# Filler matmuls joined to 512 columns and the first load split by head, in a fused attention and MLP kernel

## The chip, the cores and the metric

The kernel runs on one core of one Trainium2 chip. The core has five engines that run side by side and meet at semaphores: TensorE (PE in the profile; its weight loads are PEld), VectorE (DVE), ScalarE (ACT), GpSimd (POOL) and SyncE (SP). Sixteen DMA engines move data between the device memory and the on-chip memory. The metric is the device time of one execution in microseconds (us), as the median over runs.

## The reference

Two attentions in a row, and an MLP on what they give. For each of 8 batches and 8 heads, 32 queries p attend to 576 keys and values, and then the 576 queries q attend to the 32 rows that came out:

```python
def sm_attn(qq, kk, vv):
    s = scale * np.matmul(qq, kk.transpose(0, 1, 3, 2))
    a = np.exp(s - np.max(s, axis=-1, keepdims=True))
    a = a / (np.sum(a, axis=-1, keepdims=True) + 1e-09)
    return np.matmul(a, vv)
p_packed = sm_attn(p, k, v)              # p: (8, 8, 32, 64); q, k, v: (8, 8, 576, 64), all float32
out = sm_attn(q, p_packed, p_packed)
x = out.transpose(0, 2, 1, 3).reshape(4608, 512)
h = x @ w_in                             # (4608, 2048)
g = np.where(h >= 1, h, np.where(h <= -1, 0, (h + 1) ** 2 / 4))
return g @ w_out                         # (4608, 512), float32
```

## The kernel before

**Stages.** Each batch goes through an attention stage and a hidden stage, each pair of batches through an output stage. Attention loads k, q and v as bf16 (`load`, line 256, the cast is made by the load), transposes k and q (`trans`, on TensorE for the first three batches, line 376, and by DMA from batch 3 on, line 512), makes the scores of p against k (`scores`, line 397), exponentiates them, multiplies by v (`packed`, lines 417 and 423), makes the second scores (`weights`, line 451) with their sums (line 461), and normalises them into A (line 472). The last product of the attention isn't made: `mk` (line 493) multiplies the packed rows by w_in instead, which gives M, and a hidden tile (line 548) is M times A, for 128 of the 2,048 hidden columns at a time. Three element-wise steps (lines 553 to 563) make hT of it. An output tile (line 598) sums sixteen matmuls of hT with w_out over 128 rows.

**Order.** The order of the work on each engine is written by a planner before the program is built. `Plan.run` (line 113) holds a list of tasks with an estimated cost, the tasks on which each depends and a key; step by step it takes the task that can start first by its clock `self.now` of each engine, and emits its instructions. So the order on each engine is fixed; at run time an engine waits at the instruction that isn't ready, and all that is behind it on that engine waits too.

**Fillers.** While TensorE has nothing to do early on (until two output tiles have been begun), the planner lets it multiply zeros: in the loop, where the next TensorE task starts later than the clock by more than one filler and 0.3 us, it calls `idle()` (line 137), which emits one matmul of a 128 x 128 tile of zeros with 256 columns (`DW`) of zeros into a bank that nobody reads (line 661), and moves the clock of TensorE on by `DW / 2400` us, twice that before 4.2 us. The next pass may emit another. There are 68 of them, in runs of 13, 14, 8, 4, 1, 3, 1, 7, 3, 8 and 6 between the tasks, all within the first 20.4 us.

**Loads.** All loads of k, q, v, the weights and most of p are issued by GpSimd, one behind the other, in the order of the list that begins at `FIRST` (line 290). The first six are half loads of batch 0, four heads of eight each: k, v, q, then k, v, q of the other half. `first_loads` (line 292) issues the first three, lets GpSimd build the identity matrix that the transposes need, and issues the other three. Then follow the quarters of w_in and w_out and the loads of batch 1. From the ninth load on GpSimd waits, before it issues one, for the landing of the load eight before it. One load of four heads is 96 partitions by 4 heads by 384 values (six rows of 64).

**The start of TensorE.** Its stream begins with 13 fillers, two transposes of p (line 331, which need the identity), 14 fillers, the twelve transposes of k's first four heads, three for each head, 8 fillers, the scores of these heads, 4 fillers, and the transposes of q.

Of the kernel before, what the change touches and what calls it, by code (L numbers as in the profile page):

```python
# [14 lines left out]
         Mca=1.0, Mcd=1.22, x=0.65, ta=0.683, td=0.457, hT=0.758, oba=0.585, obd=0.69,  # L15
         array=0.2, wake=1.2, warm=4.2, early=0.3, tell=0.04, feed=0.1, slack=0.6, margin=0.15, wait=0.5)
NW, NO, NX, NB = 3, 2, 5, 6
DW = 256
TURNED = 3


# [11 lines left out]
class Plan:  # L33
# [79 lines left out]
    def run(self, idle):  # L113
        self.line = [t.seq for t in self.tasks if t.engines == ("DMA",)]
        left = {}
        given = {e: [] for e in self.ENGINES}
        for t in self.tasks:
            left[t] = len(t.deps)
            for d in t.deps:
                d.users.append(t)  # L120
            if not t.deps:
                for e in t.engines:
                    given[e].append(t)
        n = len(self.tasks)
        while n:
            best = None
            for e in self.ENGINES:
                c = self.choose(e, given, n)
                if c is not None and (best is None or c[0] < best[0]):
                    best = c[0], e, c[1]  # L130
            if self.count["O"] < 3:
                c, step = self.choose("PE", given, n), DW / 2400
                self.now["PE"] = max(self.now["PE"], C["wake"])
                if self.now["PE"] < C["warm"]:
                    step *= 2
                if (c is None or c[0] > self.now["PE"] + step + C["early"]) and best is not None and best[0] > self.now["PE"]:
                    idle()
                    self.now["PE"] += step
                    continue
            assert best is not None  # L140
            at, e, t = best
            t.on = e
            cost = t.cost[e]
            if e == "PE" and t.mode is not None and t.mode != self.mode:
                cost += C["switch"]
                self.mode = t.mode
            self.now[e] = at + cost
            t.end = at + cost + t.after + (C["land"] if e == "DMA" else 0.0)
            if e == "DMA":
                del self.line[0]  # L150
            self.log.append((at, at + cost, e, t))
            if t.takes:
                room = self.rooms[t.takes]
                t.slots = [(self.count[t.takes] + j) % len(room) for j in range(len(t.readers))]
                self.count[t.takes] += len(t.slots)
                for n_, j in zip(t.readers, t.slots):
                    room[j] = None if n_ else t.end + t.holds
            if t.frees is not None:
                f, j = t.frees
                f.gone[j] = max(f.gone[j], t.end)  # L160
                f.readers[j] -= 1
                if f.readers[j] == 0:
                    self.rooms[f.takes][f.slots[j]] = f.gone[j]
            if len(t.engines) > 1:
                t.fn(e)
            elif e in ("ACT", "DVE"):
                t.fn(e)
            else:
                t.fn()
            for x in t.engines:  # L170
                given[x].remove(t)
            for u in t.users:
                left[u] -= 1
                if left[u] == 0:
                    for x in u.engines:
                        given[x].append(u)
            n -= 1
# [3 lines left out]
def kernel(  # L181
# [10 lines left out]
    nc = tc.nc  # L192
# [9 lines left out]
    P = 128  # L202
# [30 lines left out]
    plan = Plan({"W": NW, "O": NO, "x": NX, "ob": NB})  # L233
    PE, ACT, DVE, DMA, SP = "PE", "ACT", "DVE", "DMA", "SP"
# [11 lines left out]
    zeros = const.tile([P, FW], bf16)  # L246
# [9 lines left out]
    def load(nm, b, hs):  # L256
        if (nm, b) not in tok:
            tok[nm, b] = stg.tile([TP, H, NC, D], bf16, tag=nm, name=nm)
        nc.gpsimd.dma_start(tok[nm, b][:, hs].rearrange("p h c d -> p h (c d)"),  # L259
                            SRC[nm][b, hs].rearrange("h (p c) d -> p h (c d)", c=NC))  # L260
# [29 lines left out]
    FIRST = [("k", 0), ("v", 0), ("q", 0), ("k", 1), ("v", 1), ("q", 1)]  # L290

    def first_loads():
        for nm, i in FIRST[:3]:
            load(nm, 0, HS[i])
        make_identity(nc, ident)
        for nm, i in FIRST[3:]:
            load(nm, 0, HS[i])
    for nm, i in FIRST:
        L[nm, 0, i] = add(DMA, C["half"], -1, (), (lambda: None) if L else first_loads)
# [358 lines left out]

    o = psO.tile([P, d_model], f32, tag="o", name="o")
    plan.count["O"] = 1  # L660
    plan.run(lambda: nc.tensor.matmul(o[:, :DW], zeros[:, :P], zeros[:, :DW], start=True, stop=True))  # L661


# [28 lines left out]
```

## Time and profile before

| what | value |
|---|---|
| time, median of 3 runs | 251.32 us (251.26 to 253.26) |
| the profiled execution | 250.97 us, its span from first to last instruction 249.2 us |
| granted TensorE clock | 1.00 |
| matmuls / weight loads in the profile | 2,187 / 2,220 |
| DMA moved | 34.37 MB, 138 GB/s on the mean |

The span of the profile runs from the first to the last instruction of the program; the rest of the time lies around it. Lines of a timeline read: start, duration, engine, line of the kernel, operation, tile written <- tiles read, form, count, and in brackets the idle time of the engine before it with what ended it. A wait that names a DMA ended when that load had landed. The page's busy digits of TensorE and of the DMA engines in 40 slices of 6.2 us each are:

```profile
PE   7887887999999999999999999999999999999993
...
DMA  6999999999999999999999932312112112133223
```

The first seven slices of TensorE are the only ones with holes, but for the last; the DMA engines are full to slice 23.

### The profile page before, as it was taken

The page shows a single profiled execution, that of the slowest core. Times are in us where ns is not written, and L with a number is a line of the kernel's source. Part 1 is how long each engine was busy: PE and PEld are TensorE (multiplying, and loading weights), DVE is VectorE, ACT ScalarE, POOL GpSimd, SP SyncE. Part 2 cuts the span into 40 slices and gives each one's busy share as a digit, 9 for nine tenths or more (in the row PEclk, how much of TensorE's full clock was granted, in tenths as well). Part 3 has the DMA queues.
Part 4 walks back from the last instruction along what each step waited for, and adds up shares of the span by engine and source line. Part 5 has one row for each costly group of instructions (what it writes and reads, how often), then busy time and mean ns, then how long its engine had stood idle before and what let it go on. Part 6 is the DMA issues. An engine that isn't in the chain of part 4 may idle for free.

```text
span 249.2 us, 5464 instructions
## 1 busy us (share of the span) xinstructions
PE 234.8 (94%) x2187; PEld 140.9 (57%) x2220; DVE 181.7 (73%) x308; ACT 182.5 (73%) x294; POOL 29.7 (12%) x44
## 2 busy tenths in 40 slices
PE   7887887999999999999999999999999999999993
PEld 5655465467546666556565656656556465544452
DVE  5456979788999899698979985998569878930000
ACT  3368888899888899798798984997859796841110
POOL 8632433012001301111101000000000000000000
PEclk9999999999999999999999999999999999999999
DMA  6999999999999999999999932312112112133223
GB/s 99 196 207 207 206 203 195 204 240 204 193 182 217 165 190 193 208 183 188 223 191 223 218 76 53 79 42 49 42 42 45 43 42 45 42 84 86 54 74 84
DMA packets 54825, 34.37 MB, mean 138 GB/s; under 512 B 27536, under 2 KB 50320, under 8 KB 54800
## 3 DMA queue, kind: packets, MB, share of 16 engines
q0 software_dynamic: 24672, 18.55, 49.9%
q1 hardware_dynamic: 29968, 15.34, 31.7%
q8 instruction: 17, 0.28, 0.4%
q10 hardware_dynamic: 160, 0.13, 0.2%
q14 instruction: 8, 0.07, 0.1%
HBM read 37.22 MB, written 9.44 MB: 187 GB/s over the span
## 4 chain that ended last, share of the span: by engine, by line
PE 76%; DMA 13%; ACT 3%; POOL 3%; issue 2%; DVE 2%; DVEq 0%; ACTq 0%; POOLq 0%
PE o L598 44%; PE h L548 22%; DMA w_in_sb<-in_moe_w_in_dram 7%; DMA q<-in_q_dram 6%; PE mp L493 3%; PE sp L397 2%; PE pk L417 1%; PE sm L461 1%; PE s L451 1%; PE tp L376 1%; DVE pT L319 1%; POOL w_in_sb L285 1%; ACT eT L456 1%; POOL k L259 1%; PE pk L423 1%
## 5 line engine op out<-in xcount | busy, mean ns | idle before, releaser
L598 PE MATMUL o<-w_out_sb,hT 128*128 128x512 bf16 (+1 forms) x559 | 135.6, 373 | 2.1 <-issue 1.1
L563 DVE SCALAR_TENSOR_TENSOR hT<-x 128x576 bf16<-128x576 f32 x128 | 93.2, 754 | 8.3 <-PE o L598 3.5
L598 PEld LDWEIGHTS <-hT 128*128 128x128 bf16 x592 | 56.1, 98 | 53.7 <-issue 4.8
L553 ACT ACTIVATE x<-h 128x576 f32<-128x576 f32 x128 | 77.2, 653 | 12.1 <-PE h L548 8.3
L548 PE MATMUL h<-A,M 128*128 128x288 bf16 x512 | 76.0, 286 | 1.4 <-ACT M L319 0.5
L548 PEld LDWEIGHTS <-M 128*128 128x128 bf16 x512 | 49.3, 98 | 24.1 <-ACT M L319 1.0
L558 DVE TENSOR_SCALAR x<-x 128x576 f32<-128x576 f32 x84 | 38.5, 459 | 11.8 <-ACT x L553 10.9
L319 ACT COPY ob<-o 128x512 f32<-128x512 f32 (+1 forms) x23 | 13.2, 576 | 32.1 <-PE o L598 32.1
L560 ACT ACTIVATE x<-x 128x576 f32<-128x576 f32 x44 | 29.4, 683 | 0.5
L319 DVE COPY ob<-o 128x512 f32<-128x512 f32 (+1 forms) x14 | 9.4, 669 | 25.8 <-PE o L598 25.7
L319 DVE CAST M<-mp 128x1024 bf16<-128x1024 f32 x16 | 19.4, 1218 | 2.8 <-PE mp L493 2.8
L319 ACT CAST M<-mp 128x1024 bf16<-128x1024 f32 x16 | 15.8, 1012 | 1.2 <-PE mp L493 1.2
L400 ACT ACTIVATE ex<-sp 96x768 bf16<-96x768 f32 x16 | 12.9, 806 | 3.2 <-PE sp L397 3.1
L472 DVE SCALAR_TENSOR_TENSOR A<-eT,rs,rc 128x576 bf16<-128x576 bf16 x16 | 13.0, 812 | 2.1 <-ACT rc L469 2.1
L259 POOL DMA_DIRECT2D k<-in_k_dram x10 | 7.5, 746 | 56.5 <-DMA kT<-k 40.0
L456 ACT ACTIVATE eT<-s,rs 128x576 bf16<-128x576 f32 x16 | 11.2, 736 | 2.8 <-PE s L451 2.6
L493 PE MATMUL mp<-w_in_sb,ppT 64*32 64x512 bf16 x256 | 10.7, 381 | 2.6 <-DMA w_in_sb<-in_moe_w_in_dram 2.2
L465 ACT ACTIVATE ln<-sm 128x576 f32<-128x576 f32 x16 | 10.4, 648 | 2.2 <-PE sm L461 2.1
L661 PE MATMUL o<-zeros 128*128 128x256 bf16 x68 | 10.6, 301 | 1.2 <-DVE zeros L247 1.2
L469 ACT ACTIVATE rc<-ln 128x576 f32<-128x576 f32 x16 | 10.9, 683 | 0.5
L259 POOL DMA_DIRECT2D q<-in_q_dram x10 | 7.6, 759 | 26.2 <-DMA qT<-q 12.7
L397 PEld LDWEIGHTS <-kT 128*128 128x128 bf16 x192 | 7.4, 98 | 2.6 <-DVE kT L319 0.6
(47 smaller groups left out, 114.4 us busy)
## 6 DMA issues: line engine op xcount, KB each, us to landing
out_dram<-ob SPq DMA_DIRECT2D x23, 192.0 KB, 2.5
v<-in_v_dram POOLq DMA_DIRECT2D x7, 576.0 KB, 18.4
k<-in_k_dram POOLq DMA_DIRECT2D x6, 576.0 KB, 12.4
q<-in_q_dram POOLq DMA_DIRECT2D x6, 576.0 KB, 14.0
out_dram<-ob SPq DMA_DIRECT2D x24, 128.0 KB, 2.8
w_in_sb<-in_moe_w_in_dram POOLq DMA_DIRECT2D x4, 512.0 KB, 14.7
w_out_sb<-in_moe_w_out_dram POOLq DMA_DIRECT2D x4, 512.0 KB, 16.8
out_dram<-ob SPq DMA_DIRECT2D x23, 64.0 KB, 2.0
```

The lines of the kernel that those rows point to most:

```text
L259: nc.gpsimd.dma_start(tok[nm, b][:, hs].rearrange("p h c d -> p h (c d)"), SRC[nm][b, hs].rearrange("h (p c) d -> p h (c d)", c=NC))
L319: return lambda eng: nc.vector.tensor_copy(out_, in_) if eng == DVE else nc.scalar.copy(out_, in_)
L400: nc.scalar.activation(ex()[:, :, i].rearrange("p e x a n -> p e (x a n)"), box["sp"], AF.Exp, scale=scale)
L456: nc.scalar.activation(box["eT"], box["s2"][:, :, :HALF], AF.Exp, scale=rs()[:, g, 1:])
L472: nc.vector.scalar_tensor_tensor(A()[:, g], box["eT"], rs()[:, g, :1], box["rc"], ALU.mult, ALU.mult)
L493: nc.tensor.matmul(mp[a * NP:(a + 1) * NP, g], pp_of(y, h), w_in_sb[y * D:(y + 1) * D, h // 2, f * FW:(f + 1) * FW], start=True, stop=True)
L548: nc.tensor.matmul(h[:, hf, :HALF], T[b, "M"][:, g, fi * P:(fi + 1) * P], T[b, "A"][:, g, hf], start=(g == 0), stop=(g == G - 1))
L553: nc.scalar.activation(box["x"], box["h"][:, :, :HALF], AF.Prelu, bias=-1.0, alpha=0.5)
L558: nc.vector.tensor_scalar(x, x, 1.0, 0.0, ALU.add, ALU.max)
L560: nc.scalar.activation(x, x, AF.Relu, bias=1.0)
L563: nc.vector.scalar_tensor_tensor(hT[:, fi, col:col + S].rearrange("p (a t) -> p a t", a=2), box["x"], 1.0, box["x"], ALU.min, ALU.mult)
L598: nc.tensor.matmul(o, hT[:, fi, i * P:(i + 1) * P], w_out_sb[:, fi, cs], start=(fi == 0), stop=(fi == KF - 1))
```

## The change

The planner counts the same fillers at the same places, but it emits them later: the columns are added up in `fill`, and when the next task of TensorE is emitted, matmuls of up to 512 columns (`FILL`), and one of what is left, are put ahead of it. The clock moves as before, so that the order of all tasks is the same. Of the 68 matmuls of 256 columns 37 remain, 31 of them with 512 columns and 6 with 256.

The first load, k of the first four heads, is issued in two: one head, then three. The transposes of the first head wait for the one, those of the other three for the other.

```diff
@@ -15,7 +15,7 @@
          Mca=1.0, Mcd=1.22, x=0.65, ta=0.683, td=0.457, hT=0.758, oba=0.585, obd=0.69,
          array=0.2, wake=1.2, warm=4.2, early=0.3, tell=0.04, feed=0.1, slack=0.6, margin=0.15, wait=0.5)
 NW, NO, NX, NB = 3, 2, 5, 6
-DW = 256
+DW, FILL = 256, 512
 TURNED = 3
 
 
@@ -121,7 +121,7 @@
             if not t.deps:
                 for e in t.engines:
                     given[e].append(t)
-        n = len(self.tasks)
+        n, fill = len(self.tasks), 0
         while n:
             best = None
             for e in self.ENGINES:
@@ -134,7 +134,7 @@
                 if self.now["PE"] < C["warm"]:
                     step *= 2
                 if (c is None or c[0] > self.now["PE"] + step + C["early"]) and best is not None and best[0] > self.now["PE"]:
-                    idle()
+                    fill += DW
                     self.now["PE"] += step
                     continue
             assert best is not None
@@ -161,6 +161,11 @@
                 f.readers[j] -= 1
                 if f.readers[j] == 0:
                     self.rooms[f.takes][f.slots[j]] = f.gone[j]
+
+            while e == "PE" and fill:
+                w = min(fill, FILL)
+                idle(w)
+                fill -= w
             if len(t.engines) > 1:
                 t.fn(e)
             elif e in ("ACT", "DVE"):
@@ -290,7 +295,10 @@
     FIRST = [("k", 0), ("v", 0), ("q", 0), ("k", 1), ("v", 1), ("q", 1)]
 
     def first_loads():
-        for nm, i in FIRST[:3]:
+
+        for hs in (slice(0, 1), slice(1, 4)):
+            load(FIRST[0][0], 0, hs)
+        for nm, i in FIRST[1:3]:
             load(nm, 0, HS[i])
         make_identity(nc, ident)
         for nm, i in FIRST[3:]:
@@ -658,7 +666,7 @@
 
     o = psO.tile([P, d_model], f32, tag="o", name="o")
     plan.count["O"] = 1
-    plan.run(lambda: nc.tensor.matmul(o[:, :DW], zeros[:, :P], zeros[:, :DW], start=True, stop=True))
+    plan.run(lambda w: nc.tensor.matmul(o[:, :w], zeros[:, :P], zeros[:, :w], start=True, stop=True))
 
 
 # ---- launch: one core; inputs and outputs as the reference has them ----
```

## The prediction

> **What bounds the kernel now.** I read the page first, then the chain of waits in order of time, then TensorE's own waits, and last the first microseconds row by row. The page, shares of engines and the code queue:
>
> ```profile
> PE 234.8 (94%) x2187; PEld 140.9 (57%) x2220; DVE 181.7 (73%) x308; ACT 182.5 (73%) x294; POOL 29.7 (12%) x44
> ...
> q8 instruction: 17, 0.28, 0.4%
> ...
> L661 PE MATMUL o<-zeros 128*128 128x256 bf16 x68 | 10.6, 301 | 1.2 <-DVE zeros L247 1.2
> ```
>
> TensorE is busy for 94% of the span, but that average hides two stages. The chain of waits separates them (start us, us, what):
>
> ```profile
> 8.14 16.89 DMA w_in_sb<-in_moe_w_in_dram
> 25.31 15.51 DMA q<-in_q_dram
> 40.86 0.68 PE tp L376 x12
> ...
> 219.22 10.74 PE o L598 x49
> ```
>
> Up to 40.82 us (25.31 + 15.51) the chain lies on the loads, and after that on TensorE. TensorE's waits, first for the stretch up to 41.5 us and then for what follows, say the same:
>
> ```profile
> PE mp L493 <- DMA w_in_sb<-in_moe_w_in_dram: 2.2, 3, 1.0
> PE tp L376 <- DMA q<-in_q_dram: 1.6, 3, 0.6
> ...
> PE tp L376 <- DMA k<-in_k_dram: 0.7, 2, 0.5
> ```
>
> ```profile
> PE o L598 <- issue: 1.1, 7, 0.2
> PE s L451 <- DVE qT L319: 0.4, 1, 0.4
> PE mp L493 <- DVE M L319: 0.3, 1, 0.3
> PE h L548 <- DVE pT L319: 0.3, 1, 0.3
> ```
>
> Before 41.5 us TensorE waits 4.5 us for loads (2.2 + 1.6 + 0.7); after it, for no load at all. The busy time by stretch has the same border (PE, PEld, DVE, ACT, POOL, then granted clock, DMA share, GB/s):
>
> ```profile
> 0.00:41.00 41.00, 34.17 (x416) 23.34 (x418) 27.43 (x57) 26.63 (x43) 18.52 (x30) 1.00 1.18 188
> 41.00:249.21 208.21, 200.61 (x1775) 117.61 (x1804) 154.29 (x252) 155.85 (x252) 11.19 (x14) 1.00 0.75 128
> ```
>
> So the first 41 us are one unbroken stream of loads (share 1.18, that is, packets overlap on the 16 engines), and the other 208 us are TensorE at 96% (200.61 of 208.21). The change touches the first 20 us alone, and it can move the end only by moving the moment at which the stream delivers the second half of batch 1's q, which TensorE takes up at 40.86. That is the step on which I build the sum: end = that moment + 208 us of work that the change leaves as it is.
>
> **Joined fillers.** TensorE's first instructions, in order of time (start us, us, engine, line, tiles, form, count, and in brackets the wait before):
>
> ```profile
> 1.19 2.96 PE L661 MATMUL o<-zeros 128*128 128x256 bf16 x13 [1.19 <-DVE zeros L247]
> 4.34 0.30 PE L331 MATMUL tpp<-ident,p_nat 128*128 128x128 bf16 x2 [0.19 <-DVE p_nat L328]
> 4.47 1.69 PE L661 MATMUL o<-zeros 128*128 128x256 bf16 x14
> 6.32 0.68 PE L376 MATMUL tp<-ident,k 96*128 96x96 bf16 x12 [0.16 <-DMA k<-in_k_dram]
> ...
> 9.27 0.68 PE L376 MATMUL tp<-ident,q 96*128 96x96 bf16 x12 [0.46 <-DMA q<-in_q_dram]
> ...
> 16.69 0.41 PE L493 MATMUL mp<-w_in_sb,ppT 64*32 64x512 bf16 x8 [0.65 <-DMA w_in_sb<-in_moe_w_in_dram]
> ...
> 25.07 0.41 PE L493 MATMUL mp<-w_in_sb,ppT 64*32 64x512 bf16 x8 [0.98 <-DMA w_in_sb<-in_moe_w_in_dram]
> ...
> 33.59 0.68 PE L376 MATMUL tp<-ident,k 96*128 96x96 bf16 x12 [0.51 <-DMA k<-in_k_dram]
> ...
> 40.86 0.68 PE L376 MATMUL tp<-ident,q 96*128 96x96 bf16 x12 [0.58 <-DMA q<-in_q_dram]
> ```
>
> The planner counts the same fillers between the same tasks, so each run of 256-column ones becomes half as many of 512 with one of 256 over where the count is odd: runs of 13, 14, 8, 4, 1, 3, 1, 7, 3, 8 and 6 become 7, 7, 4, 2, 1, 2, 1, 4, 2, 4 and 3. That is 68 to 37 matmuls, 31 matmuls and 31 weight loads fewer, with 17,408 columns before and after. Is a wide one cheaper than two narrow ones? The 14 took 1.69 us, and taking off one latency of 0.30 (the 301 ns of the page's row) leaves 13 steps of 0.107 us. The 512-column matmuls at the end took 10.74 / 49 = 0.219 us each. Twice 0.107 is 0.214, so the join saves nothing in array time, to within 0.005 us x 31 = 0.2 us either way, and a filler ends ahead of a wait for a load in nearly every case (0.46 at 9.27, 0.65 at 16.69 and so on), which hides even that. I take 0.
>
> What is left of this part is code: 62 instructions fewer ahead of the first real work. The code queue moved 17 pieces of 0.28 MB / 17 = 16 KB. Two of them fall into the stream of loads; each of the windows 13.3 to 14.4 and 22.9 to 24.0 us answers with this row (pieces, MB, share of 16 engines):
>
> ```profile
> q8 instruction: 1, 0.02, 5.5%
> ```
>
> 5.5% of 16 engines over 1.1 us is 0.97 us on one engine, and a load has landed only when its slowest engine is done. The Trainium skill ("Runtime: NRT & Kernel Launch", Instruction fetch mechanics) says that code comes in 16 KiB blocks of 256 instructions, fetched ahead and mostly hidden; the piece size agrees. With 62 instructions fewer the same pieces are fetched later: the first a little later, perhaps still ahead of w_in's first quarter, the second behind the third quarter of w_in, for which TensorE waits 0.98 us at 25.07. I expect that wait to shrink by up to 0.98 us. But it is not the end's: behind it stand the waits of 0.51 at 33.59 and 0.58 at 40.86, set by the stream, and they grow by what was won. On the sum: 0.
>
> **First load in two.** GpSimd's issues (start us, us, last the wait before):
>
> ```profile
> 1.28 0.80 POOL L259 DMA_DIRECT2D k<-in_k_dram  x1 [0.84 <-POOLq L676]
> 2.07 0.67 POOL L259 DMA_DIRECT2D v<-in_v_dram  x1
> 2.73 0.67 POOL L259 DMA_DIRECT2D q<-in_q_dram  x1
> ...
> 3.69 0.29 POOL masks.py:199 TENSOR_SCALAR_AFFINE_SELECT ident<-ident 128x128 bf16<-128x128 bf16 x1
> ...
> 29.76 1.22 POOL L311 DMA_DIRECT2D p_nat<-in_p_dram  x1 [1.75 <-DMA w_in_sb<-in_moe_w_in_dram]
> 32.59 0.78 POOL L259 DMA_DIRECT2D k<-in_k_dram  x1 [1.61 <-DMA w_out_sb<-in_moe_w_out_dram]
> ```
>
> A half load of four heads is 96 x 4 = 384 pieces and takes 0.67 us to issue, a whole one of 768 pieces 0.78, p's 128 x 12 = 1,536 pieces 1.22. So an issue is mostly fixed: about 0.6 us and little per piece. One head (96 pieces) then takes some 0.72 instead of the first issue's 0.80, the other three some 0.65, and v, q, the identity and all behind them are issued 0.57 us later; 0.67 if one head is no cheaper to issue. Who waits for that? The identity would be done at 4.55 rather than 3.98, so the two transposes of p start near 4.6 rather than 4.34, and the 14 fillers behind them push the first k transposes to some 6.5: 0.2 us, swallowed by the 0.46 us wait for q at 9.27. The later issues wait for the landing of the load eight before them; one more load ahead of all of them leaves each wait with the same load as before. TensorE's second wait, for heads 1 to 3, stands at the fourth of the twelve transposes; behind it are only the rest of them and fillers, and the copy to kT needs all twelve, so a head that is there early gains nothing by itself.
>
> The stream is what counts. Its start, by windows (columns as above):
>
> ```profile
> 2.80:3.40 0.60, 0.60 (x5) 0.42 (x4) 0.55 (x2) 0.00 (x0) 0.60 (x2) 1.00 0.80 55
> 3.40:4.00 0.60, 0.60 (x4) 0.20 (x2) 0.41 (x7) 0.00 (x0) 0.53 (x4) 1.00 0.82 86
> 4.00:4.60 0.60, 0.41 (x5) 0.26 (x5) 0.28 (x5) 0.00 (x0) 0.60 (x1) 1.00 1.07 161
> 4.60:5.20 0.60, 0.60 (x8) 0.54 (x6) 0.13 (x1) 0.36 (x1) 0.60 (x2) 1.00 1.28 181
> 5.20:8.80 3.60, 3.44 (x45) 2.48 (x43) 1.20 (x3) 0.75 (x2) 3.60 (x6) 1.00 1.27 190
> ```
>
> Data flow from 2.8 us, 0.7 us behind the end of the first issue (1.28 + 0.80), and climb from 55 to 190 GB/s over 2.4 us. Against a full rate this ramp lost (190 - 55 + 190 - 86 + 190 - 161 + 190 - 181) x 0.6 = 166 KB, or 0.87 us. Why it climbs no row tells. Two ends follow. If the ramp goes with the pieces of the first load, a quarter of them loses a quarter: 0.65 us won. If all loads behind the first simply start 0.57 to 0.67 us later, that is lost. Between them: one head is 288 / 4 = 72 KB as landed, which at 55 GB/s lasts 1.3 us, to 4.1; the rest of k, issued by 2.65, would have its data moving by 2.65 + 0.7 = 3.35, and v, issued by 3.3, by 4.0, when 216 KB of k are still to come. The engines do not run dry, so I take nearly nothing of the loss, and, since the issue times say that size matters little, little of the gain: the first data perhaps 0.08 us earlier (0.80 - 0.72) and some of the ramp, together 0.2 us won.
>
> The Trainium skill speaks against this edit ("DMA: Bandwidth & Descriptors", Rules for kernel authors): join small transfers, under 64 KB one pays mostly overhead; the head's 72 KB lie just above. Its fit (Anatomy of one DMA) has a fixed 2.0 us per load; taken in series that would be 253.3 us. The window 5.20 to 8.80 shows no such cost in series, three loads of 288 KB flowing at 190 GB/s; no run here shows a load of one head.
>
> **The sum.** The profiled execution took 250.97 us, 249.2 of them span, 0.35 us under the median of 251.32; the three runs go from 251.26 to 253.26. Span: 249.2 - 0 (fillers) - 0 (code) - 0.2 (stream) = 249.0, and 250.8 with what lies around it. Against the median, 251.32 - 0.2 = 251.1 us.
>
> **Rivals.** (1) Slower: GpSimd's extra issue stands ahead of every load, and the whole stream shifts by its 0.57 to 0.67 us: 251.9 to 252.0 us. For it: the chain begins with GpSimd's issues one behind the other. Against: the backlog worked out above. It decides if the 72 KB drain in under 0.55 us, before the rest of k flows (3.35 against 2.8), that is, at more than 130 GB/s. Chance 0.2. (2) Faster: the ramp shrinks with the first load, 251.32 - 0.65 = 250.7. For it: the rate climbs in step with the loads issued. Against: the flat issue times. Chance 0.2. (3) The code pieces: the 0.98 us at 25.07 falls away and is not given back at 33.59 and 40.86, 250.3 us. It would need these two waits to come from something that moves along with TensorE; the stream does not. Chance 0.05. (4) The clock: the 13 fillers took 2.96 / 13 = 0.23 us each and the 14 only 0.12, so the array runs at half speed at first, although the granted clock reads 1.00 throughout. A longer hole before the transposes of p (0.19 to some 0.5 us) might prolong that. Each filler would then cost 0.1 us more; it takes over 4.5 us of such loss to use up the waits for loads. Chance 0.03, and 254 us. (5) That the stream starts the same and nothing moves, 251.3, belongs to the forecast.
>
> **How the numbers follow.** The forecast, 251.1 us with -0.4 to +0.2 around it, has 0.5; rivals 1 to 4 have 0.2, 0.2, 0.05 and 0.03, and 0.02 is for what I have not seen. The range takes in (1) and (2) with the 0.2 us by which medians of so few runs may differ: 250.4 to 252.1. One per cent, about what a measurement of this kernel tells from no change, is 2.5 us. No case but (4) and the unseen comes near it: faster by over 1% 0.03, within 1% 0.93, slower 0.04.
>
> **What would show it.** In the profile after: 37 fillers; an issue of k of some 0.7 us and another of 0.65 ahead of v; the rate between 2.8 and 5.2 us (higher: rival 2; a hole near 3.4: rival 1); the w_in wait at 25 us shorter and the waits for k near 33.5 and q near 40.9 longer. The start of the last q transposes, 40.86 before, must move by as much as the span. If the span moves and that start does not, the border at 41 us is wrong.

## The result, and the profile after

The changed kernel took 252.59 us (median of 20 runs, 251.19 to 257.25) against 252.03 us for the kernel before beside it (20 runs, 250.83 to 253.93). The ratio is 1.004 with a 95% interval of [1.002, 1.0059] (it compares runs side by side and leaves out the two slow runs of the changed kernel, 255.36 and 257.25, so it is not the quotient of these medians): 0.5 to 1.5 us slower, and within 1%. The forecast was 251.1 us and a small gain; the time lies outside its range. The way in which it went is the first rival's. The profiled execution took 252.77 us with a span of 251.0, against 250.97 and 249.2 before.

The page after, for the busy time, the code queue and the fillers (35 of the 37 fillers are in the records):

```profile
PE 235.1 (94%) x2154; PEld 137.6 (55%) x2189; DVE 182.1 (73%) x308; ACT 182.7 (73%) x294; POOL 29.8 (12%) x45
...
q8 instruction: 17, 0.28, 0.5%
...
L669 PE MATMUL o<-zeros 128*128 128x512 bf16 (+1 forms) x35 | 10.1, 408 | 1.5 <-DVE zeros L252 1.2
```

TensorE's busy time is 0.3 us more than before although it has some 30 instructions less of each kind. So 1.5 of the 1.8 us of span are waiting. GpSimd's issues after (start us, us, last the wait before):

```profile
1.27 1.34 POOL L264 DMA_DIRECT2D k<-in_k_dram  x2 [0.82 <-POOLq L684]
2.60 0.72 POOL L264 DMA_DIRECT2D v<-in_v_dram  x1
3.31 0.67 POOL L264 DMA_DIRECT2D q<-in_q_dram  x1
...
4.27 0.29 POOL masks.py:199 TENSOR_SCALAR_AFFINE_SELECT ident<-ident 128x128 bf16<-128x128 bf16 x1
4.52 0.67 POOL L264 DMA_DIRECT2D k<-in_k_dram  x1
```

The two issues of k take 1.34 us in place of 0.80, and v, q, the identity and the next k begin 0.53 to 0.59 us later (v 2.60 against 2.07). The start of the stream, in the same windows as before (the last two columns are the share of the DMA engines and GB/s):

```profile
2.80:3.40 0.60, 0.60 (x3) 0.25 (x2) 0.55 (x2) 0.00 (x0) 0.60 (x2) 1.00 0.84 96
3.40:4.00 0.60, 0.60 (x3) 0.06 (x1) 0.41 (x7) 0.00 (x0) 0.60 (x2) 1.00 0.71 62
4.00:4.60 0.60, 0.15 (x1) 0.10 (x1) 0.35 (x5) 0.00 (x0) 0.53 (x3) 1.00 0.95 102
4.60:5.20 0.60, 0.59 (x5) 0.35 (x5) 0.00 (x0) 0.28 (x1) 0.60 (x2) 1.00 1.24 175
5.20:8.80 3.60, 3.56 (x36) 1.74 (x34) 1.33 (x3) 0.89 (x3) 3.60 (x6) 1.00 1.24 180
```

Before, these windows read 55, 86, 161, 181 and 190 GB/s. The first is better by 41; then comes a hole: 62 from 3.4 us, 102 where 161 had flowed, and from 5.2 us on still 180 in place of 190. A second profile of the changed kernel has no such hole (51, 114, 127, 186 and 162 GB/s). TensorE's first instructions, its waits for loads and one wait later on:

```profile
1.20 2.96 PE L669 MATMUL o<-zeros 128*128 128x512 bf16 x7 [1.20 <-DVE zeros L252]
4.61 0.27 PE L339 MATMUL tpp<-ident,p_nat 128*128 128x128 bf16 x2 [0.46 <-POOL ident masks.py:199]
4.72 1.67 PE L669 MATMUL o<-zeros 128*128 128x512 bf16 x7
6.23 0.72 PE L384 MATMUL tp<-ident,k 96*128 96x96 bf16 x12
...
10.05 0.68 PE L384 MATMUL tp<-ident,q 96*128 96x96 bf16 x12 [1.29 <-DMA q<-in_q_dram]
...
25.37 0.41 PE L501 MATMUL mp<-w_in_sb,ppT 64*32 64x512 bf16 x8 [0.24 <-DMA w_in_sb<-in_moe_w_in_dram]
...
34.47 0.69 PE L384 MATMUL tp<-ident,k 96*128 96x96 bf16 x12 [0.48 <-DMA k<-in_k_dram]
...
41.74 0.68 PE L384 MATMUL tp<-ident,q 96*128 96x96 bf16 x12 [0.58 <-DMA q<-in_q_dram]
...
80.23 0.52 PE L405 MATMUL sp<-pT,kT 128*128 128x64 bf16 x12 [0.17 <-DMA kT<-k]
```

The first q is taken up 0.78 us later (10.05 against 9.27), batch 1's k 0.88 later (34.47 against 33.59) and the second half of its q, the border of the prediction, 0.88 later (41.74 against 40.86). That is half of the 1.8 us. The chain of waits shows where part of the other half lies:

```profile
8.72 16.61 DMA w_in_sb<-in_moe_w_in_dram
25.61 16.08 DMA q<-in_q_dram
...
61.88 18.30 DMA kT<-k
```

The first two links are those of before, 0.9 us later at their end (25.61 + 16.08 = 41.69 against 40.82). The third is new: the DMA that transposes a later batch's k landed late, and TensorE reached the work behind it with the row at 80.23 above. Against the same instructions of the profile before, TensorE is 0.90 us late at 32 us, 1.22 behind 79 (80.23 against 79.01), 1.73 behind 135 (136.92 against 135.19) and 1.74 at the end. So the late transpose makes 0.34 of it; the other 0.51 comes at a wait for VectorE, for the packed rows of a later batch:

```profile
136.09 0.69 PE L459 MATMUL s<-qT,ppT 64*32 64x288 bf16 x16 [0.19 <-DVE ppT L441]
```

### The profile page after: what moved, and what is told of

Its sections match the earlier page's. It is cut to its first block, busy times and chain, and to the rows that moved or that the text cites. A ratio compares the mean times of both kernels' runs of the same rounds, so it can differ in the third digit from the quotient of the medians.

```text
span 251.0 us, 5401 instructions
## 1 busy us (share of the span) xinstructions
PE 235.1 (94%) x2154; PEld 137.6 (55%) x2189; DVE 182.1 (73%) x308; ACT 182.7 (73%) x294; POOL 29.8 (12%) x45
## 4 chain that ended last, share of the span: by engine, by line
PE 64%; DMA 20%; DVE 4%; ACT 4%; issue 3%; POOL 3%; DVEq 0%; ACTq 0%; POOLq 0%
PE o L606 38%; PE h L556 18%; DMA kT<-k 7%; DMA w_in_sb<-in_moe_w_in_dram 7%; DMA q<-in_q_dram 6%; PE mp L501 2%; DVE hT L571 2%; PE sp L405 1%; PE pk L425 1%; PE sm L469 1%; PE s L459 1%; PE tp L384 1%; DVE x L566 1%; ACT x L561 1%; POOL k L264 1%
## 5 line engine op out<-in xcount | busy, mean ns | idle before, releaser
L566 DVE TENSOR_SCALAR x<-x 128x576 f32<-128x576 f32 x84 | 39.1, 465 | 11.7 <-ACT x L561 11.0
L669 PE MATMUL o<-zeros 128*128 128x512 bf16 (+1 forms) x35 | 10.1, 408 | 1.5 <-DVE zeros L252 1.2
L477 ACT ACTIVATE rc<-ln 128x576 f32<-128x576 f32 x16 | 10.9, 683 | 0.5
```

What stands on the lines that cost most here:

```text
L566: nc.vector.tensor_scalar(x, x, 1.0, 0.0, ALU.add, ALU.max)
```

## The experiments

Every kernel here computes the whole reference. Diffs are against the kernel before, that of the fillers alone against the changed one. Ratios are against the kernel before in the same comparison; "taken up" is the start of TensorE's transposes of a load. Two theories stood against each other from the start: that the split costs (GpSimd hands the loads over later), or that the fillers do (code, clock, order).

**Each part alone.** The first kernel has the joined fillers and the first load whole, the second the split and fillers of 256 columns:

```diff
-        for hs in (slice(0, 1), slice(1, 4)):
-            load(FIRST[0][0], 0, hs)
-        for nm, i in FIRST[1:3]:
+        for nm, i in FIRST[:3]:
             load(nm, 0, HS[i])
```

> Joined fillers alone, first load whole. Theory A (the extra issue on GpSimd delays the stream of loads): the last q transposes of batch 1 start at 40.9 +- 0.2 us as before, first q transposes at 9.3, ratio 0.998 to 1.001. Theory B (31 fewer matmuls move the code pieces onto a slower DMA engine, and that is the loss): ratio 1.003 to 1.005, the first wait for w_in near 17.5 us instead of 16.7 although the first q transposes start at 9.3.

```diff
-        for nm, i in FIRST[:3]:
+        for hs in (slice(0, 1), slice(1, 4)):
+            load(FIRST[0][0], 0, hs)
+        for nm, i in FIRST[1:3]:
             load(nm, 0, HS[i])
```

> First load split in one head and three, 256-column fillers as before. Theory A: the whole loss, ratio 1.003 to 1.005, the first q transposes at 10.0 instead of 9.3 us and the last q transposes of batch 1 at 41.6 instead of 40.9. Theory B: ratio 1.000, q at 9.3 and 40.9.

Fillers alone: 1.0015 [0.9992, 1.0037], span 249.4, last q taken up at 41.01. Split alone: 1.0027 [1.0001, 1.0052], span 250.2, last q at 41.80, 0.94 later than before, and the end 0.92 later by TensorE's last weight loads. By the profiles the loss is the split's, and in the split's profile it goes from the border to the end as it is; the two ratios alone would not part them, since their intervals overlap. TensorE in the kernel with the fillers alone:

```profile
24.39 0.41 PE L498 MATMUL mp<-w_in_sb,ppT 64*32 64x512 bf16 x8 [0.20 <-ACT x L558]
...
30.09 0.41 PE L498 MATMUL mp<-w_in_sb,ppT 64*32 64x512 bf16 x8 [0.63 <-DMA w_in_sb<-in_moe_w_in_dram]
...
33.74 0.68 PE L381 MATMUL tp<-ident,k 96*128 96x96 bf16 x12 [0.50 <-DMA k<-in_k_dram]
```

The wait of 0.98 for the third quarter of w_in at 25.07 is gone, and the task starts 0.68 us earlier. At 30.09, where TensorE before did not wait at all (it started the same task at 30.08), it now waits 0.63 for the last quarter: the win is given back to 0.01 us, a little before the place that the prediction named. That it came from the code pieces is not shown: in the kernel with the split alone a piece of code falls into the window 23.5 to 24.5 us as it did before, and the wait at that place is as short (0.23).

**Where the cut lies.** If the extra issue alone cost, three heads and then one would cost the same as one and then three, and so would two and two; if the small first load did, a larger one would be better.

The cut is shown against the split alone:

```diff
-        for hs in (slice(0, 1), slice(1, 4)):
+        for hs in (slice(0, 3), slice(3, 4)):
```

> First load split in three heads and one instead of one and three, 256-column fillers; as many issues and the same order of bytes. If an extra issue costs by itself (theory A1): the same loss as with one and three, q at 10.0 and 41.6 us, ratio 1.003 to 1.005. If the engines run dry behind a first load that is too small (theory A2, the dip to 54 GB/s at 3.6 to 4.0 us): no dip there, q at 9.4 and 41.0 us, ratio 1.000 to 1.001.

```diff
-        for hs in (slice(0, 1), slice(1, 4)):
+        for hs in (slice(0, 2), slice(2, 4)):
```

> First load split in two heads and two. A1: first q transposes at 9.9 to 10.3 us instead of 9.3, last q transposes of batch 1 at 41.5 to 41.9. A2 (engines run dry behind a small first load): between the one-three split and no split, 9.5 and 41.2.

Three and one: 1.0055 [1.0027, 1.0082], 154 GB/s between 5 and 11 us (194 before), last q at 42.25. Two and two, a single run: 147 GB/s, last q at 42.35. Neither is better than one and three (165 GB/s, 41.80); a larger first load does not help. Part of the first kernel's span (252.0) is again a late DMA transpose, of 17.82 us from 127.98.

**One issue fewer, and a split later in the list.** The second half of k in the first load (eight heads, so the load of k behind the identity falls away); and q's second half, the sixth load, or k's, the fourth, in one and three heads instead of the first load:

```diff
-        for nm, i in FIRST[:3]:
+        load("k", 0, ALL)
+        for nm, i in FIRST[1:3]:
             load(nm, 0, HS[i])
...
-        for nm, i in FIRST[3:]:
+        for nm, i in FIRST[4:]:
```

> Both halves of batch 0's k in one load of eight heads, which is one issue fewer than before; 256-column fillers. The k transposes start 1.4 us later, near 7.7 us, and the v and q of the first four heads as much later. Theory A1: the stream gains what the extra issue lost, the last q transposes of batch 1 start at 40.0 to 40.4 us, ratio 0.996 to 0.999. Theory A2 (and any theory in which only the size of the first load counts): 40.6 to 40.9 us, ratio 0.999 to 1.001.

```diff
-        for nm, i in FIRST[3:]:
+        for nm, i in FIRST[3:5]:
             load(nm, 0, HS[i])
+        for hs in (slice(4, 5), slice(5, 8)):
+            load("q", 0, hs)
```

> First load whole; the sixth one (q, second half of the heads, issued at about 5.3 us) split in one head and three. Theory A1 (early on the writing of the loads' requests by GpSimd is what the DMA engines wait for, so every load issued in the first 9 us costs its share): k of the second half lands as before, TensorE takes it up at 10.7 +- 0.2 us, and what lies behind the split is late by 0.4 to 0.8 us: the first w_in at 17.1 to 17.5 instead of 16.7, the last q transposes of batch 1 at 41.3 to 41.7 instead of 40.9; ratio 1.002 to 1.003. Theory A3 (it is the splitting of the first load, before the stream has a backlog): 16.7 and 40.9 us, ratio 1.000.

```diff
-        for nm, i in FIRST[3:]:
+        for hs in (slice(4, 5), slice(5, 8)):
+            load("k", 0, hs)
+        for nm, i in FIRST[4:]:
             load(nm, 0, HS[i])
```

> First three loads whole; the fourth (k, second half of the heads, issued at 3.9 us, behind the identity) split in one head and three. Theory D in the form that requests written while the stream has no backlog cost: half way, 180 to 190 GB/s from 5 to 11 us, last q transposes of batch 1 at 41.0 to 41.4. If the border lies at the identity, that is at the pause of GpSimd: as with the sixth, 190 to 197 GB/s and 40.7 to 41.0.

One issue fewer: 0.9996 [0.9971, 1.002], 197 GB/s, no gain. Its profile comes from the slowest of its eleven runs (span 251.7) and has a q wait of 1.54 us at the border (41.65, which fits neither expectation), of which the ratio shows nothing. Sixth load split: 1.0001 [0.9966, 1.0037], 197 GB/s, last q at 40.67. Fourth load split: 0.999 [0.9961, 1.0019], 192 GB/s, 41.14, between the two forms of its expectation. The same cut, with the same extra issue, shows no cost here, with three or five loads handed over ahead of it; the intervals leave room for 0.9 and 0.5 us.

**The second load, and four single heads.**

```diff
-        for nm, i in FIRST[:3]:
-            load(nm, 0, HS[i])
+        load("k", 0, HS[0])
+        for hs in (slice(0, 1), slice(1, 4)):
+            load("v", 0, hs)
+        load("q", 0, HS[0])
```

> First load whole; the second one (v, first half of the heads) split in one head and three. If any extra load among the first three costs, whatever its place (theory D: GpSimd writes more requests while the stream starts): as with the first split, slow packets between 5 and 10 us, the last q transposes of batch 1 at 41.6 to 42.2 us instead of 40.9. If it must be the first (theory F): 40.7 to 41.2.

```diff
-        for nm, i in FIRST[:3]:
+        for h in range(4):
+            load("k", 0, slice(h, h + 1))
+        for nm, i in FIRST[1:3]:
             load(nm, 0, HS[i])
```

> First load in four single heads, three issues more than before. Theory D: the loss grows with the issues, two to three times that of one split, the last q transposes of batch 1 at 42.8 to 44 us, ratio 1.007 to 1.012. Theory F (a split first load costs once): 41.8 to 42.4 us, ratio 1.003 to 1.006.

Second load split: 1.0002 [0.9971, 1.0034], though its profile has 172 GB/s and the last q at 42.13; inconclusive, for the interval leaves room for 0.9 us and the profile comes from the second slowest of its ten runs. Four single heads of k put v off by 1.30 us (3.37 against 2.07): 1.0037 [1.0005, 1.0069], 156 GB/s, last q at 42.81. By the profile that is 1.95 us at the border for three issues more, twice the loss of one; the timed ratio is no worse than the change's.

**Giving the time back behind the split.** The split as in the change, with k's second half ahead of the identity, so that this load is issued at 3.97 as before (3.93); and the identity between the two parts of k:

```diff
-        for nm, i in FIRST[:3]:
+        for hs in (slice(0, 1), slice(1, 4)):
+            load(FIRST[0][0], 0, hs)
+        for nm, i in FIRST[1:3]:
             load(nm, 0, HS[i])
+        load("k", 0, HS[1])
         make_identity(nc, ident)
-        for nm, i in FIRST[3:]:
+        for nm, i in FIRST[4:]:
```

> First load split in one head and three, as in the change, but GpSimd builds the identity matrix behind the fourth load (k, second half) instead of ahead of it, so that this load is issued 0.55 us earlier; 256-column fillers. A1 with GpSimd's own time as the limit: most of the loss comes back, k of the second half is taken up at 10.8 to 11.1 us instead of 11.5, the last q transposes of batch 1 at 41.0 to 41.4 instead of 41.8. A3: nothing comes back, 11.5 and 41.8.

```diff
-        for nm, i in FIRST[:3]:
-            load(nm, 0, HS[i])
+        load("k", 0, slice(0, 1))
         make_identity(nc, ident)
+        load("k", 0, slice(1, 4))
+        for nm, i in FIRST[1:3]:
+            load(nm, 0, HS[i])
```

> First load in one head and three, with the identity matrix built by GpSimd between the two issues, so that the engines are sure to have nothing to do for a while after the first head. If running dry at the start is what costs (A2): worse than the one-three split without it, the last q transposes of batch 1 later than 41.9, towards 42.5. If not, as without it, 41.6 to 41.9; the transposes of p no longer wait for the identity.

Identity later: 1.0044 [1.0015, 1.0074], 156 GB/s, last q at 42.22: nothing is given back, so what matters lies ahead of the fourth load. Identity between: a single run, 253.55 us, 77 GB/s between 2.5 and 5 us (104 before), last q at 42.82. The first of the two also shows on TensorE what a late identity does:

```profile
5.27 0.37 PE L335 MATMUL tpp<-ident,p_nat 128*128 128x128 bf16 x2 [1.12 <-POOL ident masks.py:199]
5.44 3.19 PE L665 MATMUL o<-zeros 128*128 128x256 bf16 x14
8.43 1.17 PE L380 MATMUL tp<-ident,k 96*128 96x96 bf16 x12
```

Behind a wait of 1.12 us the 14 fillers take 3.19 us in place of 1.69, and the twelve transposes 1.17 in place of 0.68. That is the array at about half speed, the fourth rival's mechanism; at the border this kernel is 1.36 us late, which the slower stream accounts for as well, so its part cannot be told apart.

**Scatter of one profile.** Before and after once more, one profile each:

> The kernel before, unchanged, for the scatter of one profile against another. All theories: first q transposes at 9.3 +- 0.1 us, the last q transposes of batch 1 at 40.9 +- 0.2.

> The changed kernel once more, for the scatter of one profile against another: first q transposes at 9.9 to 10.2 us, the last q transposes of batch 1 at 41.6 to 41.9 in every theory in which the split shifts the stream.

Before: span 249.6, 188 GB/s, last q at 41.21. After: span 251.0, 169 GB/s, last q at 41.65. A start taken from one profile is uncertain by some 0.35 us, so single profiles here decide only differences well above that, and a single late landing, as with one issue fewer, can add more.

**Which of two: an extra load, or a later hand-over?** The last two kernels part them. The one has as many loads as before and a first load of one head, but the second brings seven:

```diff
-        for nm, i in FIRST[:3]:
+        for hs in (slice(0, 1), slice(1, 8)):
+            load("k", 0, hs)
+        for nm, i in FIRST[1:3]:
             load(nm, 0, HS[i])
         make_identity(nc, ident)
-        for nm, i in FIRST[3:]:
+        for nm, i in FIRST[4:]:
```

> Batch 0's k in one head and seven: a small first load, but as many loads as before. If the number of loads at the start counts (theory D): as the kernel with one issue fewer, 190 to 200 GB/s from 5 to 11 us, the last q transposes of batch 1 at 40.7 to 41.2 us, ratio 0.998 to 1.001. If any load of few pieces at the start slows the stream (theory S): 150 to 180 GB/s and 41.6 to 42.3 us, ratio 1.003 to 1.005.

The other has no split and no further load; it only lets GpSimd build the identity behind the first load, and so hands v and q over later:

```diff
-        for nm, i in FIRST[:3]:
-            load(nm, 0, HS[i])
+        load("k", 0, HS[0])
         make_identity(nc, ident)
+        for nm, i in FIRST[1:3]:
+            load(nm, 0, HS[i])
```

> No split and no extra load; GpSimd builds the identity matrix (0.5 us) behind the first load instead of behind the third, so that the second and the third load are issued as much later as in the change, and the fourth as before. If what counts is how early the second and third load are handed over (theory H): slow as with the split, 150 to 183 GB/s from 5 to 11 us, the last q transposes of batch 1 at 41.6 to 42.3 us, ratio 1.003 to 1.005. If it is the extra load itself (theory N): 188 to 202 GB/s and 40.7 to 41.2, ratio 0.998 to 1.001.

One and seven: 1.0002 [0.9971, 1.0032], last q at 40.63. Identity second: 1.004 [1.0016, 1.0065], medians 252.33 against 251.53, last q at 42.00, span 250.4. That is the loss of the change, without its split. (The granted clock fell in this profile from 10.9 to 17.7 us; the last q is still waited for, 0.59 us, so the border is set by the stream.) GpSimd in this kernel:

```profile
1.29 0.80 POOL L259 DMA_DIRECT2D k<-in_k_dram  x1 [0.84 <-POOLq L677]
...
2.62 0.68 POOL L259 DMA_DIRECT2D v<-in_v_dram  x1
3.30 0.67 POOL L259 DMA_DIRECT2D q<-in_q_dram  x1
3.96 0.67 POOL L259 DMA_DIRECT2D k<-in_k_dram  x1
```

v and q begin as late as in the change (2.60 and 3.31 there), and the fourth load is back at its old time. The window from 5 to 11 us, for the kernel before, for this one and for one and seven (columns as in the windows above, with TensorE's clock third from the end):

```profile
5.00:11.00 6.00, 5.24 (x85) 4.05 (x84) 2.33 (x6) 1.47 (x4) 4.71 (x8) 1.00 1.28 194
```

```profile
5.00:11.00 6.00, 4.08 (x61) 3.33 (x59) 1.33 (x3) 1.21 (x3) 4.31 (x7) 0.99 1.19 161
```

```profile
5.00:11.00 6.00, 5.36 (x63) 4.02 (x62) 1.33 (x3) 1.54 (x3) 4.92 (x8) 1.00 1.31 202
```

The stream with the late v and q moves (194 - 161) x 6 = 198 KB less in these 6 us, which at 194 GB/s is 1.02 us, and the border moves by 1.14. The DMA engines are not idle in it (1.19 against 1.28): the rate falls by 17%, the share by 7% only, so each byte holds an engine longer. One and seven issues v and q still later (2.71 and 3.40) and keeps its rate. What it shares with the kernel before is how much has been handed over by 2.75 us: 576 KB as landed, eight heads, at 2.73 (1.26 + 1.47) and at 2.74 (2.07 + 0.67). In the change and in the kernel with the identity second that amount is reached at 3.32 and 3.30.

All of them by that measure (576 KB handed over at; GB/s from 5 to 11 us; last q of batch 1 taken up; ratio):

| kernel | 576 KB at | GB/s | last q | ratio [95%] |
|---|---|---|---|---|
| one issue fewer | 2.17 | 197 | 41.65 | 0.9996 [0.9971, 1.002] |
| one and seven | 2.73 | 202 | 40.63 | 1.0002 [0.9971, 1.0032] |
| before / again | 2.74 / 2.75 | 194 / 188 | 40.86 / 41.21 | 1 |
| sixth load split | 2.74 | 197 | 40.67 | 1.0001 [0.9966, 1.0037] |
| fillers alone | 2.76 | 197 | 41.01 | 1.0015 [0.9992, 1.0037] |
| fourth load split | 2.76 | 192 | 41.14 | 0.999 [0.9961, 1.0019] |
| identity second | 3.30 | 161 | 42.00 | 1.004 [1.0016, 1.0065] |
| second load split | 3.31 | 172 | 42.13 | 1.0002 [0.9971, 1.0034] |
| split alone | 3.31 | 165 | 41.80 | 1.0027 [1.0001, 1.0052] |
| after / again | 3.32 / 3.31 | 183 / 169 | 41.74 / 41.65 | 1.004 [1.002, 1.0059] |
| split, identity later | 3.32 | 156 | 42.22 | 1.0044 [1.0015, 1.0074] |
| three and one | 3.34 | 154 | 42.25 | 1.0055 [1.0027, 1.0082] |
| two and two | 3.37 | 147 | 42.35 | one run |
| identity between | 3.84 | 155 | 42.82 | one run |
| four singles | 4.08 | 156 | 42.81 | 1.0037 [1.0005, 1.0069] |

Seven profiles reach the amount by 2.76 us and have 188 to 202 GB/s; ten reach it from 3.30 on and have 147 to 183. Between 3.3 and 4.1 the rate hardly depends on it. Batch 1's k, taken up before that q, parts the same two groups without exception: 33.35 to 33.93 us in the seven, 34.36 to 35.54 in the ten. The measure was found after these runs and is not the only one that parts them: three half loads, 864 KB, are handed over by 3.42 us in the seven and from 3.96 on in the ten. No kernel is faster than the kernel before beyond its interval.

## Why the prediction was wrong

**The step that failed** is the price of the later hand-over: "The engines do not run dry, so I take nearly nothing of the loss". That loss came in full. In place of 0.2 us won, the border moved by 0.88 us in the profile of after, 0.79 in the one taken again and 0.94 with the split alone (0.35 less each against the kernel before taken again), and the ratio says 0.5 to 1.5 us. The reckoning under it missed in the profile of after: it had one head's 72 KB last 1.3 us at 55 GB/s and the rest of k flow by 3.35, but 2.8 to 3.4 ran at 96 GB/s and the next two windows at 62 and 102. More than that, running dry is not what decides. One and seven has the same hole and loses nothing:

```profile
2.80:3.40 0.60, 0.60 (x5) 0.41 (x4) 0.55 (x2) 0.00 (x0) 0.60 (x2) 1.00 0.88 93
3.40:4.00 0.60, 0.60 (x4) 0.20 (x2) 0.41 (x7) 0.00 (x0) 0.60 (x2) 1.00 0.76 53
4.00:4.60 0.60, 0.14 (x1) 0.10 (x1) 0.43 (x5) 0.00 (x0) 0.53 (x4) 1.00 1.09 101
4.60:5.20 0.60, 0.51 (x4) 0.44 (x4) 0.00 (x0) 0.10 (x1) 0.60 (x2) 1.00 1.12 172
```

By 5.2 us it is (55 + 86 + 161 + 181 - 93 - 53 - 101 - 172) x 0.6 = 38 KB behind the kernel before, after's profile 29 KB and the one of after taken again 3 KB, while the kernel with the identity second (82, 96, 173 and 175 GB/s) is 26 KB ahead and still loses 1.14 us. What the runs show in place of that step is a stream that goes on more slowly from 5 to 11 us, with its engines busy, when its first loads are handed over half a microsecond later. In the split alone this window makes (194 - 165) x 6 = 174 KB, 0.90 us at 194 GB/s, and in after taken again 150 KB, 0.77 us: the whole delay of the border. In the profile of after itself the two windows make 29 and 66 KB, 0.49 of the 0.88 us; the rest is in no row shown here.

**The base.** Of the 1.49 us between the forecast and the measured time 0.71 are the kernel before itself, 252.03 us beside the changed one against 251.32 in the three runs on which the forecast stood. What is wrong with the forecast is its direction.

**The first rival** came closest: the later hand-over through GpSimd's extra issue, and the direction, with a chance of 0.2. Its 0.57 to 0.67 us lie inside the interval of the ratio and at or below what the profiles show. What it had wrong is the way. It is no plain shift of the whole stream by the length of an issue: with the identity second only v and q come later, the fourth load and all behind it are on time, and the loss is there. Nor is the extra issue needed, or "a hole near 3.4" a sign of the loss. Its point of decision, 130 GB/s, was not reached (96).

**The size of the load.** The Trainium skill ("DMA: Bandwidth & Descriptors", Rules for kernel authors) says to join small transfers, since under 64 KB one pays mostly overhead; that spoke against the edit and had the right side. The runs do not bear out that ground: one and seven heads has the same first load of 72 KB and no loss, and three and one loses as well.

**Right, by rows.** Fillers at nothing: 7 matmuls took the 2.96 us of 13, the next 7 1.67 against 1.69, and the interval of the fillers alone holds 1. The win at 25 us without worth at the end: won 0.68, given back by 30.1. The identity "at 4.55" ended at 4.56 (4.27 + 0.29), p's transposes began at 4.61 (forecast 4.6) and k's at 6.23 (6.5). v was issued at 2.60, 0.53 later (0.57). Code moved later as said, 17 pieces again. One reading was short: not two but three pieces fall into the stream of loads before; the window 39.8 to 40.9 us, just ahead of the border, answers with the same row. With the fillers alone that piece comes behind the border (at 41.76), and the last q is no earlier (41.01), so nothing hangs on it. Within 1%, to which 0.93 was given, held.

**Half right: the border at 41 us.** In the split alone the delay at the border and at the end agree (0.94 and 0.92), with the identity second too (1.14, and 1.2 in the span). In the profile of after another 0.86 us came behind it, at the two waits named with the result, for a transposed k (80.23) and for VectorE (136.09). The first of these tasks in the split alone, which is as late at the border:

```profile
79.94 0.51 PE L400 MATMUL sp<-pT,kT 128*128 128x64 bf16 x12
```

There it waits for nothing, and TensorE stays 0.92 us late to the end. So "208 us of work that the change leaves as it is" has waits in it with little slack, and some executions lose there what others do not. What made VectorE late is not shown.

**Open:** why a stream whose first 576 KB are handed over half a microsecond later moves 147 to 183 GB/s until 11 us. Its bytes hold the engines longer; part of that may be that more k, q and v and less of w_in lies in the window. And whether splitting the second load, with the same delay and the same slow stream in its profile, really costs nothing. The ratio shows no loss, but its three runs with a mean granted clock above 0.993 took 251.90 to 252.40 us, the nine such runs of before beside it 251.03 to 251.89, so the loss may be there and lie under the scatter.

## What to carry to other kernels

In this kernel, whose first stage waits for a stream of loads, an issue or an identity put among the first three loads held the next ones back by about 0.55 us and cost that or more at the border (0.8 to 1.1 us against one profile of before, 0.35 less against the other); the same issue at the fourth or the sixth load showed no cost. Handing over more and sooner won nothing (one issue fewer). Before a load is split, ask how much has been handed over while the first bytes move, not whether the piece is big enough or whether the engines run dry. Time won on an engine that waits for a stream is given back at the next landing, so a shorter wait in the profile is no gain until the last of those landings has moved.

## What was not expected of the hardware

The granted clock can fall inside the part that was taken as rigid. In the profile of after taken again, two windows behind the border (the clock is the third number from the end):

```profile
41.13:44.54 3.41, 2.07 (x46) 1.26 (x46) 3.09 (x6) 2.75 (x4) 1.53 (x2) 1.00 1.67 187
44.54:47.95 3.41, 3.41 (x31) 0.74 (x24) 2.77 (x3) 2.35 (x4) 0.00 (x0) 0.50 1.34 205
```

The clock reads 0.50 for 3.41 us, and groups of eight matmuls for M take 0.63 us in place of 0.41. TensorE is 0.80 us late at 32 us and 1.8 at the end. Within the first 50 us eight of the 17 profiles have such a fall, of 3.41 us or twice that: beginning between 42 and 45 us also with the second load split, the identity between, one issue fewer and the sixth load split, and between 10.9 and 16.7 us with three and one, the second load split, the fourth load split and the identity second. Both profiles of before have none there. The Trainium skill ("TensorE: Matmul & The Clock Gate", Part 1: The HAM clock gate) gives half rate as the state after an idle window of about 3.4 us, the windows running free of the kernel. The length agrees with that; but TensorE was not idle ahead of this fall, it was busy for 2.07 of the 3.41 us. Nor does it take a late stream: with the sixth load split q came at 40.67 and the clock fell all the same, at 42.74.

How often it falls is told by the mean clock of each timed run: one fall of 3.41 us makes it 1 - 0.5 x 3.41 / 250 = 0.993. Of the 104 runs of the kernel before that stand beside the experiments 42 have 0.993 or less, with a median of 252.33 us; the other 62 have a median of 251.25. So a good part of the scatter of before goes with the clock. In the six experiments with a late hand-over that were timed more than once, 43 of 64 runs have 0.993 or less, in the five others 16 of 53. The loss is there without it too (four single heads: 252.60 us in the median of seven runs above 0.993, against 251.18 in nine of before beside them), but part of the cost of a late stream may come through the clock; that it does is not shown.
